# An attention and soft-MoE kernel: its decays computed in two halves at the opening, and its second layers taken in pairs of experts at the end

## The chip, the cores and the metric

The kernel runs on one core of a Trainium2 chip. The metric is the device time of one execution in microseconds (us), the median of three runs. Engines are called as the profile calls them: PE is TensorE's matmul and PEld its weight load, DVE is VectorE, ACT is ScalarE, POOL is GpSimd, and SP is SyncE, which issues every DMA of this kernel in one order.

## What is computed

The input is attention over 8 batches and 8 heads of 576 positions by 64, with a decay, and a soft mixture of 8 experts with 4 slots each on its output:

```python
log_f = np.log(np.clip(f, 0.0001, 1.0))
cum = np.cumsum(log_f, axis=-1)
scores = np.where(causal, -1e9, scale * q @ k.T + cum[:, :, :, None] - cum[:, :, None, :])
attn = softmax(scores) @ v                      # x: 4608 tokens x 512
logits = x @ phi                                # 4608 x 32 slots
slot_input = softmax_over_tokens(logits).T @ x  # 8 experts x 4 slots x 512
for e in range(8):
    slot_out[e] = np.maximum(slot_input[e] @ w1[e], 0.0) @ w2[e]
out = softmax_over_slots(logits) @ slot_out     # 4608 x 512, f32, 9.44 MB
```

## The kernel before

The order of work on each engine is the written order of the program; the framework adds the semaphores. All arithmetic is f32 or fp32r (f32 rounded for TensorE's fast path). Where more exactness is wanted, a number is used as a rounded part (hi) and the remaining part (lo).

**Opening (0 to about 26 us).** `f` (64 rows of 576) lands in `PTS`. DVE clips it (L548), ACT takes its logarithm (L549), DVE sums it along the row by a scan (L553), rounds the sums (L562) and takes the remaining part (L563, L564). ACT and DVE put sum rows into `WA[0]`, and fill rows into `YA[0]`. The keys and queries of pair 0 are in `RAW[0]`; `round_k` (L183) rounds a head's keys into `WA`, `round_q` (L188) its queries into `YA`, both on ACT. `dup_k` (L199) and `dup_q` (L203) are DMAs that copy these into `WB` and `YB`; `low_k` (L209) and `low_q` (L214) on POOL then write the remaining parts beside them. `s1` (L230) multiplies queries by keys for the row maxima, `tops` (L244, L246) takes the maxima on DVE, `s2` (L283, L284) makes the transposed scores with the maximum in them, `expo` (L290) their exponentials on ACT, `s3` (L315) the products with the values, `norm` (L330 to L335) the division. `warm` (L516) are matmuls on constants.

**Middle.** 32 pairs of heads run through a software pipeline of these steps; weights of the experts are loaded between them.

**End (from about 325 us).** `mlp1` and the first half of the second layers (`mlp2(e, 0)`, 16 matmuls each) run while weights still arrive. The output has two column halves of 256. For a half n, `gathered(n)` copies the sum of all experts out of PSUM, `slots(n)` adds up the four parts by a matmul with `srep`, and `halve(n)` makes the rounded and remaining part in `SO`. `blocks(n0, n1, half)` makes one or two blocks of 128 tokens by 256 columns, copies them out of PSUM on ACT and DVE in turn (L1071), and issues their DMA to the output (L1073), 256 KB for two blocks. There are 36 blocks in each half. Half 0's blocks are interleaved with the eight `mlp2(e, 1)`, which make half 1, and with the transposes of later batches' weights (`more`, L723). Of half 1, all blocks stand behind `halve(1)`.

Of the kernel before, what the change touches and what calls it, by code (L numbers as in the profile page):

```python
# [15 lines left out]
B, H, S, D = 8, 8, 576, 64  # L16
NE, SPE, DM, DF = 8, 4, 512, 1024
# [4 lines left out]
NBLK = 5  # L22
EPS = 1e-9

WARM = (11, 1)

CUM = ((64, 96), (64, 65), (64, 65))
TOP = (97, 66, 66)
# [41 lines left out]
SIDES = [[x for n in zip(units(h, 0, range(4)), units(h, 1, range(4))) for x in n] for h in range(2)]  # L70
LAST = [units(h, h, (4,)) for h in range(2)]
# [3 lines left out]
def attn_softmoe(ctx: ExitStack, tc: tile.TileContext, qk, v, f, phi, w1, w2, cst, out):  # L75
    nc = tc.nc
# [21 lines left out]
    YA, WA, YB, WB = {}, {}, {}, {}  # L98
# [204 lines left out]
    def blank(h):  # L303

        t = pv[h][:, 0:325].rearrange("p (t e) -> p t e", e=65)
        lanes = slice(64 * (1 - h), 64 * (1 - h) + 64)
        nc.vector.memset(t[lanes, 4, 0:64], 0.0)
        nc.vector.memset(t[lanes, 4, 64:65], 1.0)
        return t

    def s3(g, todo):
        for h, t, u, c in todo:
            r = queries(t, u)
            at = pt_col(c, 64 * r)
# [7 lines left out]
    def norm(i):  # L322
        if not head(i):
            return
        g, h = divmod(i, 2)
        b, p = divmod(g, NPAIR)
        x, o = xtile(b, p // 2), pvv[h]
        at = 128 * (p % 2) + 64 * h
        rl = small.tile([P, NBLK], F32, name=f"rl{i}", tag="rl")
        nc.vector.tensor_scalar_add(rl, o[:, :, 64], EPS)  # L330
        nc.vector.reciprocal(rl, rl)
        rl = rl.rearrange("p (t o) -> p t o", o=1)
        for ts in (slice(0, NBLK),) if i < NH - 1 else (slice(0, NBLK, 4), slice(1, 4)):
            to = x[:, ts, at : at + 64]
            nc.vector.tensor_tensor(to, o[:, ts, 0:64], rl[:, ts].broadcast_to(list(to.shape)), op=ALU.mult)  # L335
# [177 lines left out]
    def warm(n, a, w=192):  # L513

        for _ in range(n):
            nc.tensor.matmul(ring[0][:, 0:w], a[:, 0:128], a[:, 0:w], start=True, stop=True)  # L516
# [18 lines left out]
        nc.vector.memset(t[64:128, 448:512], 0.0)  # L535

    fill = V.rearrange("p a t c -> p (a t c)")[:, 0:1280].bitcast(F32R)
    nc.vector.memset(fill[0:1].bitcast(F32), -1.0)
    for h in range(2):
        nc.scalar.mul(fill[32:34, 640 * h : 640 * h + 640], fy[32:34], -8.0)  # L540
    warm(WARM[0], fy)
    nc.gpsimd.memset(WA[0][64:96].bitcast(F32), 0.0)
    nc.gpsimd.memset(YA[0][64:98].bitcast(F32), -8.0)
    nc.gpsimd.memset(WA[0][96:98].bitcast(F32), -1.0)
    nc.gpsimd.memset(YA[0][0:64, :, 0:64].bitcast(F32), 0.0)
    nc.gpsimd.memset(LG[:, 128:256], -1.0e30)
# [12 lines left out]
    dup_q(0, 0, 1)
    round_k(0, 1)  # L560

    nc.vector.tensor_copy(fp[lane, 0:S], fz)  # L562
    nc.vector.tensor_tensor(WA[0][96:97, 0:S], fz[0:1], fp[64:65, 0:S].bitcast(F32), op=ALU.subtract)  # L563
    nc.vector.tensor_tensor(fp[lane, S:], fz, fp[lane, 0:S].bitcast(F32), op=ALU.subtract)  # L564
    for m in (1, 2):
        nc.sync.dma_start(WA[m][66:67].bitcast(F32), fill[0:1, 0 : 2 * S].bitcast(F32))
        nc.sync.dma_start(YA[m][64:66].rearrange("c h s -> c (h s)").bitcast(F32), fill[32:34].bitcast(F32))
        if m == 1:
            dup_k(0, 1, 2)
            for c in range(2):  # L570
                nc.sync.dma_start(WA[1][64 + c : 65 + c].bitcast(F32), fp[65:98:32, S * c : S * c + S].bitcast(F32))
            nc.sync.dma_start(cumd.rearrange("b a c s -> (b a) (c s)"), fp[lane].bitcast(F32))
    for h in range(2):
        nc.scalar.copy(WA[0][64:65, S * h : S * h + S], fp[64 + 32 * h : 65 + 32 * h, 0:S])  # L574
    nc.scalar.copy(WA[0][96:97, S:], fp[96:97, S:])
    round_q(0, 1)
    dup_q(0, 1, 2)
    nc.scalar.activation(fin[:, 0:1], ones[:, 0:1], AF.Exp)
    for h in range(2):
        low_k(h)  # L580
        low_q(h)
    for m in (1, 2):
        nc.gpsimd.memset(YA[m][0:64, :, 0:64].bitcast(F32), 0.0)
    nc.gpsimd.memset(fin[0:1, 4:5], -1.0)
# [496 lines left out]
    mlp2(0, 1)
    slots(0)
    halve(0)
    mlp2(1, 1)
    more(5)
    ring += [po[0], bank[0]]
    runs = (((0, 2), (2, 4), (4, 6)), ((6, 8), (18, 20), (20, 22)), ((22, 24), (24, 26), (8, 9)), ((26, 27), (9, 11), (11, 13)), ((13, 15), (15, 17), (17, 18)), ((27, 29), (29, 31)), ((31, 33), (33, 35), (35, 36)))
    turns = ((5, 2), (2, 3), (3, 6), (6, 7), (7,), ())
    for e in range(2, NE):
        for n in runs[e - 2]:  # L1090
            blocks(*n, half[0])
        if e == 3:
            split(7, 0, 1)
        mlp2(e, 1)
        for n in turns[e - 2]:
            more(n)
    gathered(1)
    for n in runs[-1]:
        blocks(*n, half[0])
    slots(1)  # L1100
    halve(1)
# [45 lines left out]
```

## Time and profile before

| | |
|---|---|
| time, median of 3 runs | 384.83 us (384.54 to 384.94) |
| profiled execution, its own time | 384.53 us |
| its span, first to last instruction | 382.8 us |
| mean granted TensorE clock | 0.989 |
| busy: PE, DVE, ACT, POOL | 96%, 74%, 71%, 67% |
| instructions | 15236 |

The profiled execution lies 0.30 us below the median; 1.7 us of its time are outside the span. Busy shares are means over stages with different limits: in the middle PE is busy nearly always, and in the last eight fortieths of the span the DMA engines are.

### The profile page before, as it was taken

The numbers are of one execution on the slowest core, as the hardware profiler recorded it, in microseconds if no ns is written. First come the engines' busy times: TensorE is split into PE (matmuls) and PEld (weight loads), VectorE is DVE, ScalarE is ACT, GpSimd is POOL, SyncE is SP. The second block draws the span as 40 slices with busy tenths as digits, with TensorE's granted clock in tenths as the row PEclk, the third lists the DMA queues.
The fourth block names the chain that finished last, engine by engine and source line by source line (L and its number), as shares of the span: only waits on it lengthen the run. The fifth ranks groups of instructions, "written<-read, shape, count | busy, mean of one in ns | idle before, by whom it ended". The sixth has DMA issues, their size and how long they took to land.

```text
span 382.8 us, 15236 instructions
## 1 busy us (share of the span) xinstructions
PE 365.8 (96%) x5904; PEld 328.5 (86%) x5904; DVE 285.0 (74%) x1078; ACT 270.8 (71%) x656; POOL 257.0 (67%) x364
## 2 busy tenths in 40 slices
PE   7999999999999999999999999999999999999950
PEld 7899999999999999999999999999999986556650
DVE  7878887887888888888888888888888636442670
ACT  8969887878787878787878787878787653112450
POOL 4987887878797879787978797879787941010000
PEclk9999999999999999999999999999999999999995
DMA  6785878677768777778777777777777889999998
GB/s 209 202 200 158 240 231 272 197 221 214 236 188 242 206 233 210 219 205 235 214 218 215 224 212 221 216 220 217 218 217 210 264 290 395 411 406 374 313 330 293
DMA packets 37480, 93.72 MB, mean 245 GB/s; under 512 B 4458, under 2 KB 14368, under 8 KB 37408
## 3 DMA queue, kind: packets, MB, share of 16 engines
q1 hardware_dynamic: 37408, 92.75, 78.6%
q8 instruction: 46, 0.75, 0.8%
q14 instruction: 26, 0.21, 0.2%
HBM read 63.93 MB, written 9.73 MB: 192 GB/s over the span
## 4 chain that ended last, share of the span: by engine, by line
PE 91%; DVE 2%; ACT 1%; DMA 1%; issue 1%; POOL 0%; DVEq 0%; POOLq 0%; ACTq 0%
PE pv L315 25%; PE ring L283 15%; PE s L230 13%; PE ring L284 13%; PE pv L342 4%; PE lg L389 3%; PE pv L992 2%; PE ds L480 2%; PE ring L961 2%; PE pv L961 2%; PE ring L992 2%; PE ring L1070 1%; PE ring L480 1%; DMA PTS<-in_f 1%; PE more L1070 1%
## 5 line engine op out<-in xcount | busy, mean ns | idle before, releaser
L290 ACT ACTIVATE PTS<-ring 128x320 f32<-128x320 f32 (+2 forms) x256 | 119.4, 500 | 37.6 <-PE ring L284 29.9
L283 PE MATMUL ring<-YA,WA 67*128 67x320 f32 (+9 forms) x384 | 119.0, 324 | 0.0
L246 DVE CUSTOM_DVE_ANT_0 s<-s,mask 128x320 f32<-128x320 f32 (+3 forms) x256 | 109.5, 446 | 6.1 <-PE s L230 0.7
L284 PE MATMUL ring<-YB,WB 128*128 128x320 f32 (+4 forms) x384 | 110.5, 296 | 0.0
L315 PE MATMUL pv<-V,PTS 128*64 128x65 f32 x3200 | 101.9, 223 | 0.1
L315 PEld LDWEIGHTS pv<-V,PTS 128*64 128x64 f32 x3200 | 96.9, 138 | 3.0 <-issue 1.3
L230 PE MATMUL s<-WA,YA 66*128 66x288 f32 (+9 forms) x384 | 97.9, 311 | 1.0 <-ACT WA L574 0.6
L209 POOL TENSOR_TENSOR WB<-RAW,WB 64x576 fp32r<-64x576 f32 x64 | 90.7, 1417 | 10.3 <-DMA YA<-V 5.1
L214 POOL TENSOR_TENSOR YB<-RAW,YA 64x576 fp32r<-64x576 f32 x64 | 89.7, 1421 | 2.6
L283 PEld LDWEIGHTS ring<-YA,WA 67*128 67x128 f32 (+3 forms) x384 | 69.0, 181 | 5.4 <-issue 2.1
L284 PEld LDWEIGHTS ring<-YB,WB 128*128 128x128 f32 (+1 forms) x384 | 70.0, 182 | 0.0
L230 PEld LDWEIGHTS s<-WA,YA 66*128 66x128 f32 (+1 forms) x384 | 62.9, 190 | 6.5 <-ACT WA L574 0.8
L246 DVE DVE_READ_ACCUMULATOR2_ANT MT<- 128x1 fp32r x310 | 44.0, 142 | 0.0
L301 POOL TENSOR_SCALAR_AFFINE_SELECT PTS<-PTS 128x128 f32<-128x128 f32 (+1 forms) x128 | 31.3, 265 | 17.8 <-ACT PTS L290 14.7
L183 ACT CAST WA<-RAW 64x576 fp32r<-64x576 f32 x64 | 40.2, 669 | 3.7 <-DMA RAW<-in_qk 2.8
L298 POOL TENSOR_SCALAR_AFFINE_SELECT PTS<-PTS 128x384 f32<-128x384 f32 x64 | 33.3, 521 | 12.8 <-ACT PTS L290 7.4
L188 ACT CAST YA<-RAW 64x576 fp32r<-64x576 f32 x64 | 40.8, 669 | 0.4
L246 DVE CUSTOM_DVE_ANT_0 s<-s,mask,MT 128x288 f32<-128x288 f32 x62 | 32.6, 526 | 10.0 <-PE s L230 1.4
L342 PE MATMUL pv<-cs,X 128*128 128x128 f32 x155 | 36.5, 272 | 0.0
L335 DVE TENSOR_TENSOR X<-pv,rl 128x320 f32<-128x320 f32 (+1 forms) x65 | 31.5, 486 | 2.4 <-DMA YA<-mr 0.3
L330 DVE TENSOR_SCALAR rl<-pv 128x5 f32<-128x5 f32 x64 | 10.5, 164 | 26.4 <-PE pv L315 21.2
L244 DVE TENSOR_REDUCE MT<-s 128x1 fp32r<-128x288 f32 x62 | 28.0, 451 | 0.5
(257 smaller groups left out, 382.3 us busy)
## 6 DMA issues: line engine op xcount, KB each, us to landing
w<-in_w SPq DMA_DIRECT2D x45, 512.0 KB
RAW<-in_qk SPq DMA_DIRECT2D x31, 576.0 KB
V<-in_v SPq DMA_DIRECT2D x32, 325.0 KB
YB<-YA SPq DMA_DIRECT2D x30, 288.0 KB
WB<-WA SPq DMA_DIRECT2D x30, 288.0 KB
p<-in_w SPq DMA_DIRECT2D x6, 512.0 KB
out<-RAW SPq DMA_DIRECT2D x12, 256.0 KB
out<-p SPq DMA_DIRECT2D x10, 256.0 KB
```

The lines of the kernel that those rows point to most:

```text
L183: nc.scalar.copy(WA[g % 3][0:64, S * h : S * h + S], RAW[g % 3][64:128, h])
L188: nc.scalar.copy(YA[g % 3][0:64, h, 64:640], RAW[g % 3][0:64, h])
L209: nc.gpsimd.tensor_tensor(t[0:64], RAW[g % 3][64:128, h], t[64:128].bitcast(F32), op=ALU.subtract)
L214: nc.gpsimd.tensor_tensor(YB[g % 2][64:128, h], RAW[g % 3][0:64, h], YA[g % 3][0:64, h, 64:640].bitcast(F32), op=ALU.subtract)
L230: nc.tensor.matmul(t[:, o : o + w], ya[0:m, h, 128 * blk : 128 * blk + 128], wa[0:m, j0 : j0 + w], start=True, stop=True)
L246: nc.vector.tensor_tensor_reduce(out=t[:, o : o + w], in0=t[:, o : o + w], in1=mask[:, m0 : m0 + w], scale=1.0, scalar=top.bitcast(F32) if ...
L283: nc.tensor.matmul(o, wa[0:m, j0 : j0 + n], ya[0:m, h, 64 + i0 : 64 + i0 + w], start=True, stop=False)
L284: nc.tensor.matmul(o, wb[:, j0 : j0 + n], yb[:, h, i0 : i0 + w], start=False, stop=True)
L290: nc.scalar.activation(PT[i % 2][:, SEG_O[bank] : SEG_O[bank] + at], t[:, 0:at], AF.Exp, scale=0.125)
L298: nc.gpsimd.affine_select(d3, d3, pattern=[[0, 3], [1, 128]], compare_op=ALU.is_ge, fill=0.0, base=0, channel_multiplier=-1)
L315: nc.tensor.matmul(pvv[h][64 * u : 64 * u + 64, t, :], PT[h][:, at : at + 64], V[:, g % 2, c, 65 * h : 65 * h + 65], start=(c == 0), stop= ...
L342: nc.tensor.transpose(pm[:, 0:128], x[:, t, 128 * (p % 2) : 128 * (p % 2) + 128], ident)
```

## The change

Opening:
- The clip, the logarithm and the scan are done in two column halves of 288. The second scan starts from the last sum of the first. Two memsets of DVE stand ahead of the clip now.
- The fill rows of `YA[0]` are written by ACT rather than POOL, and the fill data for the other tiles are spread over 9 and 20 partitions.
- Nine warm matmuls stand at the start rather than 11.
- The load of the next pair's keys and queries (`load_qk(1)`, 576 KB) is issued behind the first `dup_k` and `dup_q` rather than ahead of them.
- The queries of head 1 are rounded on POOL, between `low_k(0)` and `low_q(0)`, rather than on ACT. ACT's copy of a sum row (L574 before, L566 now) stands ahead of `round_k(0, 1)`.
- `first(2, 2)` stands before the last part of head 0's `s2`; `norm(0)` stands behind `first(4, 3)`, and `s3` of head 1 is not split any more.

End:
- `gathered` makes a rounded part (ACT) and a remaining part (DVE) in two column halves of 128, and POOL copies `srep` beside them. `slots` is two fp32r matmuls (hi and lo) rather than one f32 matmul. `halve` does its two steps for each column half of 128.
- The second layers of half 1 run in pairs of experts, `runs` regroups the blocks in four groups, and `more` does four transposes groups at a time. `gathered(1)` stands right behind `mlp2(7, 1)`, ahead of the group of blocks from 27 on; `slots(1)` and `halve(1)` stand before the block pair (33, 35).

```diff
-    load_qk(1)
...
     for h in range(2):
-        nc.scalar.mul(fill[32:34, 640 * h : 640 * h + 640], fy[32:34], -8.0)
+        nc.scalar.mul(YA[0][64:98, h], fy[64:98], -8.0)
...
-    nc.gpsimd.memset(YA[0][64:98].bitcast(F32), -8.0)
...
-    nc.vector.tensor_scalar(fx, fx, 1e-4, 1.0, op0=ALU.max, op1=ALU.min)
-    nc.scalar.activation(fx, fx, AF.Ln)
...
-    nc.vector.tensor_tensor_scan(fz, fy[lane, 0:S], fx, 0.0, ALU.mult, ALU.add)
+    parts = slice(0, S // 2), slice(S // 2, S)
+    for n in parts:
+        nc.vector.tensor_scalar(fx[:, n], fx[:, n], 1e-4, 1.0, op0=ALU.max, op1=ALU.min)
+        nc.scalar.activation(fx[:, n], fx[:, n], AF.Ln)
+    for n, start in zip(parts, (0.0, fz[:, S // 2 - 1 : S // 2])):
+        nc.vector.tensor_tensor_scan(fz[:, n], fy[lane, n], fx[:, n], start, ALU.mult, ALU.add)
...
     dup_k(0, 0, 1)
     dup_q(0, 0, 1)
-    round_k(0, 1)
+    load_qk(1)
...
+    nc.scalar.copy(WA[0][64:65, 0:S], fp[64:65, 0:S])
+    round_k(0, 1)
...
-    round_q(0, 1)
+    low_k(0)
+    nc.gpsimd.tensor_copy(YA[0][0:64, 1, 64:640], RAW[0][0:64, 1])
     dup_q(0, 1, 2)
     nc.scalar.activation(fin[:, 0:1], ones[:, 0:1], AF.Exp)
-    for h in range(2):
-        low_k(h)
-        low_q(h)
+    low_q(0)
+    low_k(1)
+    low_q(1)
...
     s3(0, SIDES[0][20:] + LAST[0])
-    norm(0)
     first(4, 1)
-    s3(0, LAST[1] + SIDES[1][:8])
     first(4, 2)
     first(4, 3)
-    s3(0, SIDES[1][8:])
+    norm(0)
+    s3(0, LAST[1] + SIDES[1])
...
+    parts = [slice(128 * n, 128 * n + 128) for n in range(2)]
+    room = [last[0][:, 0:640], CW[0].rearrange("p t o r s -> p (t o r s)")]
+
     def gathered(n):
 
-        nc.vector.tensor_copy(so[:, half[n]], po[n][:, 0:256])
+        nc.gpsimd.tensor_copy(room[n][:, 512:640], srep)
+        for c in parts:
+            hi, lo = room[n][:, c], room[n][:, 256 + c.start : 256 + c.stop]
+            nc.scalar.copy(hi, po[n][:, c])
+            nc.vector.tensor_tensor(lo, po[n][:, c], hi.bitcast(F32), op=ALU.subtract)
 
     def slots(n):
-        nc.tensor.matmul(pr[n], srep, so[:, half[n]], start=True, stop=True)
+        for k in range(2):
+            nc.tensor.matmul(pr[n], room[n][:, 512:640], room[n][:, 256 * k : 256 * k + 256], start=(k == 0), stop=(k == 1))
 
     def halve(n):
-        nc.scalar.copy(SO[:, half[n]], pr[n])
-        nc.vector.tensor_tensor(SO[64:128, half[n]], pr[n][64:128], SO[64:128, half[n]].bitcast(F32), op=ALU.subtract)
+        for c in parts:
+            to = SO[:, 256 * n + c.start : 256 * n + c.stop]
+            nc.scalar.copy(to, pr[n][:, c])
+            nc.vector.tensor_tensor(to[64:128], pr[n][64:128, c], to[64:128].bitcast(F32), op=ALU.subtract)
...
-    runs = (((0, 2), (2, 4), (4, 6)), ((6, 8), (18, 20), (20, 22)), ((22, 24), (24, 26), (8, 9)), ((26, 27), (9, 11), (11, 13)), ((13, 15), (15, 17), (17, 18)), ((27, 29), (29, 31)), ((31, 33), (33, 35), (35, 36)))
...
+    runs = (
+        ((0, 2), (2, 4), (4, 6), (6, 8)),
+        ((18, 20), (20, 22), (22, 24), (24, 26), (8, 9), (26, 27)),
+        ((9, 11), (11, 13), (13, 15), (15, 17), (17, 18)),
+        ((27, 29), (29, 31), (31, 33), (33, 35), (35, 36)),
+    )
+    turns = ((5, 2), (3, 6), (7,), ())
...
+    for e in range(0, NE, 2):
+        mlp2(e, 1)
+        if e == 0:
+            slots(0)
+            halve(0)
+            ring += [po[0], bank[0]]
+        mlp2(e + 1, 1)
+        if e == NE - 2:
+            gathered(1)
+        for n in runs[e // 2]:
+            if n == (33, 35):
+                slots(1)
+                halve(1)
             blocks(*n, half[0])
-        if e == 3:
+        for n in turns[e // 2]:
+            more(n, 4)
+        if e == 0:
             split(7, 0, 1)
```

The first place is POOL's start of the opening's remaining parts, before and then after, with the semaphores that each row waits for (WB and YB take the remaining parts, RAW_95 is pair 0, DMAHW is a DMA's).

```order
L209 TENSOR_TENSOR WB_92<-RAW_95,WB_92 64x576 [waits DMAHW6_49,DMAHW1_49]
L214 TENSOR_TENSOR YB_91<-RAW_95,YA_89 64x576 [waits Activation_49,Pool_49]
L209 TENSOR_TENSOR WB_92<-RAW_95,WB_92 64x576 [waits DMAHW2_49]
L214 TENSOR_TENSOR YB_91<-RAW_95,YA_89 64x576 [waits Activation_49]
L583 MEMSET YA_85 64x2x64
```

```order
L209 TENSOR_TENSOR WB_92<-RAW_95,WB_92 64x576 [waits DMAHW5_49,DMAHW1_49]
L580 CAST YA_89<-RAW_95 64x576 [waits DMAHW2_49]
L214 TENSOR_TENSOR YB_91<-RAW_95,YA_89 64x576 [waits Activation_49,Pool_49]
L209 TENSOR_TENSOR WB_92<-RAW_95,WB_92 64x576 [waits DMAHW2_49]
L214 TENSOR_TENSOR YB_91<-RAW_95,YA_89 64x576 [waits Pool_49]
```

The rounding of head 1's queries (L580) now stands behind POOL's first instruction, which waits for the DMA of `dup_k`.

The second place is ACT at the first fold of the end, before and then after (ring and more are PSUM banks, SO takes the folded slots, RAW_95 an output block).

```order
L1055 CAST SO<-ring_151 128x256 [waits PE_49]
L733 CAST cT<-more_5701 128x256 [waits PE_49]
L1071 COPY RAW_95<-more_5702 128x512 [waits DMAHW3_49,DVE_49,PE_49]
L1071 COPY RAW_96<-ring_150 128x512 [waits DMAHW2_49,DVE_49,PE_49]
L733 CAST cT_6032<-ring_152 128x256 [waits DVE_49,PE_49]
```

```order
L1057 CAST cT_6033<-ring_152 128x128 [waits PE_49]
L1057 CAST cT_6033<-ring_152 128x128 [waits DVE_49]
L1067 CAST SO<-ring_151 128x128 [waits PE_49]
L1067 CAST SO<-ring_151 128x128 [waits DVE_49]
L1083 COPY RAW_95<-more_5702 128x512 [waits DMAHW3_49,PE_49]
```

The second column half's rounding on ACT now waits for DVE, at `gathered` (L1057) and again at `halve` (L1067).

The third place is DVE at the second fold, before and then after (w and p are output blocks).

```order
L1049 COPY ctok<-pv_148 128x256 [waits PE_49]
L1071 COPY w_131<-ring_150 128x512 [waits PE_49,Activation_49]
L1071 COPY w_138<-ring_152 128x256 [waits PE_49]
L1056 TENSOR_TENSOR SO<-pv_149,SO 64x256 [waits Activation_49]
L1071 COPY RAW_95<-more_5702 128x512 [waits DMAHW7_49,PE_49]
```

```order
L1058 TENSOR_TENSOR cw_5634<-pv_148,cw_5634 128x128 [waits Activation_49] x2
L1083 COPY w_130<-more_5703 128x512 [waits PE_49]
L1083 COPY w_131<-ring_150 128x512 [waits PE_49]
L1068 TENSOR_TENSOR SO<-pv_149,SO 64x128 [waits Activation_49] x2
L1083 COPY w_138<-ring_151 128x256 [waits PE_49]
L1083 COPY RAW_95<-more_5703 128x512 [waits DMAHW7_49,PE_49]
```

Behind `gathered(1)` now stand four and a half output pieces of half 0, where one and a half stood before; the first of them is copied by DVE behind the two subtractions.

## Rows read from the trace of the kernel before

**Rows 1.** The page: granted clock by fortieths of the span, and the chain's shares.

```profile
PEclk9999999999999999999999999999999999999995
...
PE 91%; DVE 2%; ACT 1%; DMA 1%; issue 1%; POOL 0%; DVEq 0%; POOLq 0%; ACTq 0%
```

**Rows 2.** The chain at the opening: start us, us, what.

```profile
0.81 2.64 DMA PTS<-in_f
...
3.47 0.92 DVE PTS L548
...
4.42 0.69 ACT PTS L549
...
5.13 1.36 DVE PTS L553
...
6.52 0.47 DVE PTS L562
...
10.68 0.54 PE s L230 x3
```

**Rows 3.** The timeline of the opening: start us, us, engine line op, [idle before <-releaser].

```profile
5.81 0.52 SPq L199 DMA_DIRECT2D WB<-WA  x1
...
7.20 1.36 ACT L574 CAST WA<-PTS 1x576 fp32r<-1x576 f32 x2
...
9.85 1.41 POOL L209 TENSOR_TENSOR WB<-RAW,WB 64x576 fp32r<-64x576 f32 x1 [5.09 <-DMA YA<-V]
```

**Rows 4.** Groups by line and form: busy us, mean ns of one.

```profile
L1071 DVE COPY p<-ring 128x512 f32<-128x512 f32 x4 | 2.7, 684 | 0.1
...
L1071 DVE COPY w<-ring 128x256 f32<-128x256 f32 x2 | 0.8, 416 | 0.0
...
L335 DVE TENSOR_TENSOR X<-pv,rl 128x128 f32<-128x128 f32 x1 | 0.3, 292 | 0.0
...
L730 ACT CAST cT<-more 128x128 fp32r<-128x128 f32 x2 | 0.4, 269 | 0.4 <-PE more L721 0.4
...
L298 POOL TENSOR_SCALAR_AFFINE_SELECT PTS<-PTS 128x384 f32<-128x384 f32 x64 | 33.3, 521 | 12.8 <-ACT PTS L290 7.4 <-ACT XTS L375 1.2 <-POOL WB L209 0.3
...
L432 POOL COPY LDT<-LDT 32x64 f32<-32x64 f32 x7 | 1.6, 226 | 0.4
```

**Rows 5.** The chain around the first products with the values.

```profile
23.07 1.19 PE pv L315 x26
...
24.82 0.85 PE pv L315 x24
```

**Rows 6.** The timeline of the end: start us, us, engine line op.

```profile
347.89 0.42 DVE L1049 COPY ctok<-ring 128x256 f32<-128x256 f32 x1 [3.83 <-PE ring L992]
...
348.61 0.70 PE L1052 MATMUL ring<-ctok,cs 128*128 128x256 f32 x2
...
349.35 0.37 ACT L1055 CAST SO<-ring 128x256 fp32r<-128x256 f32 x1 [5.89 <-PE ring L1052]
349.75 0.43 DVE L1056 TENSOR_TENSOR SO<-ring,SO 64x256 fp32r<-64x256 f32 x1 [1.44 <-ACT SO L1055]
...
363.38 0.43 DVE L1049 COPY ctok<-pv 128x256 f32<-128x256 f32 x1 [0.35 <-PE pv L992]
...
366.03 0.59 ACT L1071 COPY w<-ring 128x512 f32<-128x512 f32 x1 [1.06 <-PE ring L1070]
```

**Rows 7.** The chain at the end: second layers without and with a switch, and blocks.

```profile
340.41 0.86 PE ring L992 x16
...
362.32 1.00 PE pv L992 x16
...
366.00 0.24 PE more L1070 x2
```

**Rows 8.** Windows of the end: us, busy time of each engine, granted clock, DMA share, GB/s.

```profile
378.00:381.00 3.00, 0.00 (x0) 0.00 (x0) 0.00 (x0) 0.00 (x0) 0.00 (x0) 0.50 1.02 343
381.00:382.80 1.80, 0.00 (x0) 0.00 (x0) 0.00 (x0) 0.00 (x0) 0.00 (x0) 0.50 0.23 77
```

More of the change, by code (lines that the diff above doesn't have):

```diff
@@ L23 @@
 EPS = 1e-9
-WARM = (11, 1)
+WARM = (9, 1)
 CUM = ((64, 96), (64, 65), (64, 65))
@@ L537, in attn_softmoe @@
     fill = V.rearrange("p a t c -> p (a t c)")[:, 0:1280].bitcast(F32R)
-    nc.vector.memset(fill[0:1].bitcast(F32), -1.0)
+    nc.vector.memset(fill[0:9, 0:128].bitcast(F32), -1.0)
     for h in range(2):
-        nc.scalar.mul(fill[32:34, 640 * h : 640 * h + 640], fy[32:34], -8.0)
+        nc.scalar.mul(YA[0][64:98, h], fy[64:98], -8.0)
+    for h in range(2):
+        nc.vector.memset(m2[h], -8.0)
+    pvv = [blank(h) for h in range(2)]
     warm(WARM[0], fy)
+    nc.gpsimd.memset(fill[32:52, 0:128].bitcast(F32), -8.0)
     nc.gpsimd.memset(WA[0][64:96].bitcast(F32), 0.0)
-    nc.gpsimd.memset(YA[0][64:98].bitcast(F32), -8.0)
     nc.gpsimd.memset(WA[0][96:98].bitcast(F32), -1.0)
@@ L547, in attn_softmoe @@
     nc.gpsimd.memset(EX[:, 192:256], 0.0)
-    nc.vector.tensor_scalar(fx, fx, 1e-4, 1.0, op0=ALU.max, op1=ALU.min)
-    nc.scalar.activation(fx, fx, AF.Ln)
-    for h in range(2):
-        nc.vector.memset(m2[h], -8.0)
-    pvv = [blank(h) for h in range(2)]
-    nc.vector.tensor_tensor_scan(fz, fy[lane, 0:S], fx, 0.0, ALU.mult, ALU.add)
+    parts = slice(0, S // 2), slice(S // 2, S)
[4 more added lines that the diff above has]
+        nc.vector.tensor_tensor_scan(fz[:, n], fy[lane, n], fx[:, n], start, ALU.mult, ALU.add)
     round_k(0, 0)
@@ L559, in attn_softmoe @@
     dup_q(0, 0, 1)
-    round_k(0, 1)
+    load_qk(1)
     nc.vector.tensor_copy(fp[lane, 0:S], fz)
     nc.vector.tensor_tensor(WA[0][96:97, 0:S], fz[0:1], fp[64:65, 0:S].bitcast(F32), op=ALU.subtract)
+    nc.scalar.copy(WA[0][64:65, 0:S], fp[64:65, 0:S])
+    round_k(0, 1)
     nc.vector.tensor_tensor(fp[lane, S:], fz, fp[lane, 0:S].bitcast(F32), op=ALU.subtract)
     for m in (1, 2):
-        nc.sync.dma_start(WA[m][66:67].bitcast(F32), fill[0:1, 0 : 2 * S].bitcast(F32))
-        nc.sync.dma_start(YA[m][64:66].rearrange("c h s -> c (h s)").bitcast(F32), fill[32:34].bitcast(F32))
+        nc.sync.dma_start(WA[m][66:67].bitcast(F32), fill[0:9, 0:128].bitcast(F32))
+        nc.sync.dma_start(YA[m][64:66].rearrange("c h s -> c (h s)").bitcast(F32), fill[32:52, 0:128].bitcast(F32))
         if m == 1:
@@ L572, in attn_softmoe @@
             nc.sync.dma_start(cumd.rearrange("b a c s -> (b a) (c s)"), fp[lane].bitcast(F32))
-    for h in range(2):
-        nc.scalar.copy(WA[0][64:65, S * h : S * h + S], fp[64 + 32 * h : 65 + 32 * h, 0:S])
+    nc.scalar.copy(WA[0][64:65, S:], fp[96:97, 0:S])
     nc.scalar.copy(WA[0][96:97, S:], fp[96:97, S:])
-    round_q(0, 1)
+    low_k(0)
+    nc.gpsimd.tensor_copy(YA[0][0:64, 1, 64:640], RAW[0][0:64, 1])
     dup_q(0, 1, 2)
     nc.scalar.activation(fin[:, 0:1], ones[:, 0:1], AF.Exp)
-    for h in range(2):
-        low_k(h)
-        low_q(h)
+    low_q(0)
+    low_k(1)
+    low_q(1)
     for m in (1, 2):
@@ L632, in attn_softmoe @@
     next(r1)
+    first(2, 2)
     s2(0, 3, 4, 5)
@@ L639, in attn_softmoe @@
     load_cum(2)
-    first(2, 2)
     first(2, 3)
@@ L1002, in attn_softmoe @@
     half = [slice(256 * n, 256 * n + 256) for n in range(2)]
-    so = ctok.rearrange("p b t s -> p (b t s)")[:, 0:DM]
     used = 0
@@ L1078, in more @@
             next(c[b])
-    gathered(0)
[L1081 to L1086, printed above, removed]
-    runs = (((0, 2), (2, 4), (4, 6)), ((6, 8), (18, 20), (20, 22)), ((22, 24), (24, 26), (8, 9)), ((26, 27), (9, 11), (11, 13)), ((13, 15), (15, 17), (17, 18)), ((27, 29), (29, 31)), ((31, 33), (33, 35), (35, 36)))
-    turns = ((5, 2), (2, 3), (3, 6), (6, 7), (7,), ())
-    for e in range(2, NE):
-        for n in runs[e - 2]:
+    runs = (
[4 rows of a table added]
+    )
+    turns = ((5, 2), (3, 6), (7,), ())
+    gathered(0)
+    for e in range(0, NE, 2):
[11 more added lines that the diff above has]
+                halve(1)
             blocks(*n, half[0])
-        if e == 3:
+        for n in turns[e // 2]:
+            more(n, 4)
+        if e == 0:
             split(7, 0, 1)
[L1094 to L1101, printed above, removed]
     ring += [po[1], bank[1]]
```

## The prediction

> **What bounds the kernel now.** I read the page first, then the chain of waits, then the timelines of the two stretches that the change touches, then windows of the end. Nine tenths of the chain that ended last are PE's [rows 1]: from the first scores to the last second layer, time that PE loses or wins goes to the end, whatever the other engines do. Two stretches differ. Before 10.7 us the chain has no PE: the load of f, the clip, the logarithm, the scan and the rounding follow each other on DVE and ACT with hardly a gap [rows 2], and nothing can start earlier than these end. At the end the output's DMA decides: in its last microseconds no engine works, and the DMA engines write 343 GB/s at a full share [rows 8]. A piece of two blocks is 256 KB (262,144 bytes), so 0.764 us. Data end at 381.00 + 77 x 1.80 / 343 = 381.40 us. Half 1's first piece is out of PSUM at 366.03 + 0.59 = 366.62 [rows 6]; its 18 pieces take 13.75 us, so 1.03 us pass from ready to first byte: 366.62 + 1.03 + 13.75 = 381.40. The reader should see that the end is set by when the last long unbroken train of pieces starts, and by how many pieces are in it.
>
> **Opening: the decays in halves.** A DVE copy of 512 columns takes 0.684 and one of 256 columns 0.416 us [rows 4], so about 0.15 us of an instruction don't shrink; the same follows for ACT from 0.59 and 0.37 [rows 6]. Halves are then 0.53 for the clip, 0.42 for the logarithm, 0.75 for the scan. With f landed at 3.45 [rows 2]: clips 3.47 to 4.00 and to 4.53, logarithms 4.03 to 4.45 and 4.56 to 4.98, scans 4.56 to 5.31 and to 6.06. Before, the scan ended at 6.49: 0.4 us won for the rounding, for ACT's row copy (before held to 7.20 behind a rounding that is now behind it [rows 3]) and for head 0's first scores.
>
> **Opening: what this runs into.** Head 1's scores (10.68 [rows 2]) need its rounded queries. These are now made by POOL behind its first `low_k`, which waits for `dup_k`: issued at 5.81, it let POOL start only at 9.85, after 5.09 us idle [rows 3]. Now ACT's rounding ends earlier and no 576 KB load is queued ahead, so issue at 5.70. Landing is bounded by f's 2.64 us from issue to use (8.35) and by the 4.04 us of before (9.75); I take the middle, 8.9, since the two loads of pair 0 and the constants are still ahead. `low_k` takes 1.41 [rows 3]. POOL's rounding of 64x576 isn't in the trace: below stands a 32x64 copy (0.23), above the two-input 64x576 (1.41); a line through 0.23 for 64 columns and 0.52 for 384 [rows 4] gives 0.70 for 576, which I take as nearest. Head 1 then starts at 8.9 + 1.41 + 0.70 + 0.04 = 11.05, 0.4 us later than before. With the ends of both bounds it is 10.4 to 12.6, so -0.3 to +1.9. Behind the waiting `low_k` on POOL stand `low_q(0)` (end 8.9 + 1.41 + 0.70 + 1.41 = 12.4; before 9.85 + 2 x 1.41 = 12.7), then head 1's parts. So the 0.4 us of the halves are not spent where they arise: head 0 is early, head 1 late, and PE takes them in order.
>
> **Opening: the rest.** Moving `norm(0)` and joining `s3` of head 1: 26 products took 1.19 and 24 took 0.85 on the chain [rows 5], 46 and 35 ns each; at the lower rate 0.3 are saved. `first(4, 3)` now has a bank of tops ahead of it, so I take -0.2 (0 to -0.5). Nothing for the smaller memsets, the fill rows on ACT (it waits for DVE there anyway), fewer warm matmuls (PE's clock was granted at nine tenths or more in every fortieth but the last [rows 1]), and the fill DMAs. The moved load adds one issue of about 0.5 us on SP ahead of the fills and the second `dup_k`; their readers stand behind three POOL instructions. If its 576 KB are late for the next pair's rounding, ACT waits, inside the upper bound. Opening: +0.4 - 0.2 = **+0.2 us** (-0.8 to +1.9).
>
> **End: the folds.** Before, `gathered` is one DVE copy of 0.42, hidden beside a second layer, and `halve` 0.37 on ACT, then 0.43 on DVE [rows 6]. Now each is ACT, DVE, ACT, DVE, because ACT's second part waits for DVE's first (the order shows the wait): 0.27 + 0.29 + 0.27 + 0.29 [rows 4], with four hand-overs of 0.03 to 0.04 (349.35 + 0.37 to 349.75 [rows 6]) **1.26 us**. If instead ACT's second part followed its first at once, the fold would be 0.27 + 0.27 + 0.29 and two hand-overs, 0.9 us. In the trace, DVE never starts on a bank before ACT is done with it (349.72, 349.75 [rows 6]), so it shows no overlap within one bank.
> The Trainium skill's page PSUM — Partial Sum Buffer, section "PSUM bank collisions raise a hardware error", says that two engines may not touch one bank in the same 32 partitions at once, reads and different columns included, and that the chip does not hold one back, so that a dependency is added. By it a fold is the 1.26 us; without it, 0.9. No run so far shows a collision.
>
> **End: PE up to the last second layer.** Before: 347.85 to 363.32 [rows 6, 7], 15.47 us. Now: idle before `slots`, 347.85 + 1.26 = 349.11 instead of 348.58, +0.53; `slots` as two matmuls at block rate (0.24 for two [rows 7]) instead of about 0.65, -0.4; `mlp2(1, 1)` runs to 350.4 and `halve` to 349.4 + 1.26 = 350.7, +0.3 (before, transposes filled this); 27 blocks rather than 31 ahead of `mlp2(7, 1)`, -4 x 0.12 = -0.5; second layers in pairs save a switch (1.00 against 0.86 [rows 7]) three times, -0.4. Sum -0.5: `mlp2(7, 1)` ends at **362.9**.
>
> **End: the train of pieces.** `gathered(1)` holds DVE and ACT to 362.9 + 1.26 = 364.1, and the copy of blocks 27 and 28 stands behind it on DVE: ready at 364.85. By then the queue has run dry: the first 13.5 pieces take 10.3 us from about 352.6, to 362.9. All that is left is 4.5 pieces of half 0 and 18 of half 1, 22.5 x 0.764 = 17.2 us, in one train: 364.85 + 1.03 + 17.2 = 383.1, against 381.40, **+1.7 us**. Half 1 can't be late: `halve(1)` ends near 365.7, and the 4.5 pieces last to 369.3. So the hold that stood before half 1 moves to 4.5 pieces earlier and lasts longer. Bounds: with no saving from pairs +2.1, with folds of 0.9 us +0.7, with folds that cost no more than before (no idle, 0.43) 0.
>
> **Sum.** 384.53 + 0.2 + 1.7 = **386.4 us** for the profiled execution, whose time is 0.30 below the median of 384.83; I give it unmoved. Against the median it is 1.6 us or 0.4% more. About 0.2% (0.77 us) is what a measurement of this kernel can tell from no change.
>
> **Rivals.**
> First, *the folds overlap*: ACT's second part does not wait in practice because DVE is already done. For it: DVE's part is as short as ACT's. Against it: DVE can only begin when ACT's first part ends. Then +0.7 and 384.53 + 0.2 + 0.7 = 385.4, no change by the bound above.
> Second, on the other side, *the folds are free and the opening wins*: for it speak the 0.4 us of the halves and the 0.5 us fewer of PE before the last second layer. With folds as cheap as before, `mlp2(7, 1)` ends at 362.0, the first piece is ready at 363.2, and 363.2 + 1.03 + 17.2 = 381.4: end +0. With `dup_k` landed by 8.4 and the saving at `s3`, the opening gives -0.7: 383.8, faster. It decides from a first piece at 363.2 or earlier.
> Third, *the gate on POOL*: `dup_k` lands as late as before and the rounding costs as much as the two-input form: opening +1.7, 384.53 + 1.7 + 1.7 = 387.9. For it: the 5.09 us that POOL idled. Against it: the load ahead of `dup_k` is gone.
> That the change doesn't do what it says (halves that PE's queue swallows, so that neither end moves) gives 384.5.
>
> **How the numbers follow.** Forecast 0.53 (own range 385.6 to 387.4), folds that overlap 0.14, free folds with a winning opening 0.13, the POOL gate 0.13, neither end moves 0.07. Slower than 385.6: the forecast and the gate, 0.66; within 0.2%: overlap and no move, less a little, 0.20; faster: 0.14. The range leaves out the free folds and the worst of the gate: 384.3 to 387.8.
>
> **What would show it.** Right: the scan's second half ends near 6.1; POOL's first `low_k` starts between 8.4 and 9.7, and PE's first scores of head 1 begin right behind its rounding; four steps of 0.27 to 0.30 at each fold, ACT's second waiting for DVE; PE idle ahead of `slots`; a DMA share well below 1 between 363 and 366, then 17.2 us without a gap. Wrong: ACT's two parts back to back; a share of 1 through 363 to 366, which would mean that pieces queue up behind the DMA and the late train costs nothing; or first exponentials more than 0.5 us earlier than before.

## The result and the profile after

The changed kernel takes 386.70 us (median of 13, 386.12 to 390.66) against 384.69 for the kernel before (13 runs beside it): a ratio of 1.0064, 95% interval 1.0046 to 1.0083. It is slower by about 2 us. The profiled execution took 387.12 us, with a span of 385.4 against 382.8.

The page of the changed kernel, granted clock by fortieths, and the shares of the chain [rows 1]:

```profile
PEclk9999999999999999999999999999999999999985
...
PE 89%; DVE 2%; ACT 2%; DMA 2%; POOL 1%; issue 1%; DVEq 0%; SPq 0%; ACTq 0%; POOLq 0%
PE pv L315 25%; PE ring L283 14%; PE s L230 13%; PE ring L284 13%; PE pv L342 4%; PE lg L389 3%; PE ds L480 2%; PE ring L964 2%; PE pv L964 2%; PE ring L995 2%; PE pv L995 2%; DMA WA<-cumd 1%; ACT PTS L290 1%; PE more L1082 1%; PE ring L1082 1%
```

New in the chain is a DMA, the load of the decay sums (`WA<-cumd`, 1%). PE's share fell from 91% to 89%; DMA, ACT and POOL gained 1% each.

Its timeline of the opening answers to [rows 2, 3] (start us, us, engine line op, [idle before <-releaser]):

```profile
4.38 1.69 DVE L555 TENSOR_TENSOR_SCAN PTS<-WB,PTS 64x288 f32<-64x288 f32 x2 [0.29 <-ACT PTS L553]
...
5.58 0.53 SPq L199 DMA_DIRECT2D WB<-WA  x1
...
6.79 0.60 SPq L174 DMA_DIRECT2D RAW<-in_qk  x1
7.51 0.90 SPq L570 DMA_DIRECT2D WA<-V  x1
...
8.05 1.41 POOL L209 TENSOR_TENSOR WB<-RAW,WB 64x576 fp32r<-64x576 f32 x1 [4.34 <-DMA WB<-WA]
...
9.52 0.66 POOL L580 CAST YA<-RAW 64x576 fp32r<-64x576 f32 x1
...
10.23 0.45 PEld L230 LDWEIGHTS s<-WA,YA 97*128 97x128 f32 x3 [0.28 <-POOL YA L580]
...
11.70 0.80 SPq L570 DMA_DIRECT2D WA<-V  x1
...
13.65 1.30 ACT L290 ACTIVATE PTS<-ring 128x448 f32<-128x448 f32 x3
...
15.25 0.37 SPq L178 DMA_DIRECT2D V<-in_v  x1
...
18.27 0.45 SPq L194 DMA_DIRECT2D WA<-cumd  x1
...
20.80 1.39 PE L315 MATMUL pv<-V,PTS 128*64 128x65 f32 x40 [0.93 <-POOL YB L214]
...
22.48 0.47 PE L230 MATMUL s<-WA,YA 66*128 66x320 f32 x2 [0.29 <-DMA WA<-cumd]
...
26.39 0.47 PE L283 MATMUL ring<-YA,WA 67*128 67x448 f32 x1
```

The same view of the kernel before:

```profile
3.49 0.43 SPq L174 DMA_DIRECT2D RAW<-in_qk  x1
...
7.09 0.59 SPq L566 DMA_DIRECT2D WA<-V  x1
...
10.38 0.83 PE L230 MATMUL s<-WA,YA 97*128 97x320 f32 x3
...
10.91 0.58 SPq L566 DMA_DIRECT2D WA<-V  x1
...
13.99 1.30 ACT L290 ACTIVATE PTS<-ring 128x448 f32<-128x448 f32 x3 [0.21 <-PE ring L284]
...
14.23 0.39 SPq L178 DMA_DIRECT2D V<-in_v  x1
...
20.13 1.39 PE L315 MATMUL pv<-V,PTS 128*64 128x65 f32 x40
...
21.45 0.50 PE L230 MATMUL s<-WA,YA 66*128 66x320 f32 x2
...
25.60 0.47 PE L283 MATMUL ring<-YA,WA 67*128 67x448 f32 x1
```

The scan ends at 6.07 rather than 6.49. POOL's `low_k` starts 2.5 us after the issue of `dup_k`, and head 1's scores start right behind POOL's rounding, at 10.23 against 10.38 before. The first exponentials start at 13.65; before it was 13.99. Then PE waits twice where it did not wait before, 0.93 us ahead of the first products with the values and 0.29 for the decay sums.

The row names POOL's L214 for the first wait, but the semaphores in the trace name the load of the values (L178): its last part lands at 20.67, and PE is let go at 20.70. Before, these were 19.47 and 19.50. In run 2 below, where the row names ACT, they are 20.64 and 20.67.

So PE, 0.34 us ahead at 13.65, is 0.67 behind at the first products, and 0.79 behind the products of pair 0 (26.39 against 25.60). When the end begins, its sum of half 0 is ready 1.14 us later (349.03 below against 347.89 [rows 6]). That last part comes in the middle, most of it in one step near 43 us that no wait in the rows explains.

The timeline of the end answers to [rows 6]:

```profile
349.03 0.27 ACT L1057 CAST cT<-ring 128x128 fp32r<-128x128 f32 x1 [4.43 <-PE ring L995]
349.33 0.29 DVE L1058 TENSOR_TENSOR cT<-ring,cT 128x128 fp32r<-128x128 f32 x1 [4.12 <-ACT cT L1057]
349.65 0.27 ACT L1057 CAST cT<-ring 128x128 fp32r<-128x128 f32 x1 [0.35 <-DVE cT L1058]
349.95 0.29 DVE L1058 TENSOR_TENSOR cT<-ring,cT 128x128 fp32r<-128x128 f32 x1 [0.33 <-ACT cT L1057]
...
350.02 0.66 PE L1062 MATMUL ring<-cT 128*128 128x256 f32 x2 [0.19 <-issue]
...
363.84 0.27 ACT L1057 CAST cw<-pv 128x128 fp32r<-128x128 f32 x1 [1.48 <-PE pv L995]
...
364.76 0.29 DVE L1058 TENSOR_TENSOR cw<-pv,cw 128x128 fp32r<-128x128 f32 x1 [0.33 <-ACT cw L1057]
...
364.97 0.68 DVE L1083 COPY w<-more 128x512 f32<-128x512 f32 x1
```

ACT, DVE, ACT, DVE: each waits for the other, and a fold takes 1.21 us. The first piece of the last group is copied behind it, ready at 365.65.

Windows of the end answer to [rows 8] (granted clock, DMA share and GB/s are the last three):

```profile
365.50:366.00 0.50, 0.35 (x3) 0.14 (x2) 0.50 (x2) 0.27 (x1) 0.00 (x0) 1.00 0.65 225
366.00:366.50 0.50, 0.00 (x0) 0.00 (x0) 0.47 (x2) 0.00 (x0) 0.00 (x0) 1.00 0.06 20
366.50:367.00 0.50, 0.00 (x0) 0.00 (x0) 0.17 (x2) 0.39 (x2) 0.00 (x0) 1.00 0.83 264
...
367.50:368.00 0.50, 0.50 (x4) 0.50 (x4) 0.15 (x1) 0.00 (x1) 0.00 (x0) 0.50 1.02 352
...
383.50:384.00 0.50, 0.00 (x0) 0.00 (x0) 0.00 (x0) 0.00 (x0) 0.00 (x0) 0.50 0.77 266
```

The queue is nearly dry from 365.7 to 366.6. Then the train runs without a gap to 383.5 + 266 x 0.5 / 343 = 383.89. That is 2.49 us later than before: 1.14 from the middle and 1.35 from the end itself.

### The profile page after: what moved, and what is told of

Read it like the earlier page. It is cut to its first block, busy times and chain, and to the rows that moved or that the text cites. A ratio compares the mean times of both kernels' runs of the same rounds, so it can differ in the third digit from the quotient of the medians.

```text
span 385.4 us, 15243 instructions
## 1 busy us (share of the span) xinstructions
PE 366.3 (95%) x5900; PEld 329.9 (86%) x5900; DVE 284.1 (74%) x1084; ACT 271.7 (70%) x662; POOL 256.9 (67%) x367
## 4 chain that ended last, share of the span: by engine, by line
PE 89%; DVE 2%; ACT 2%; DMA 2%; POOL 1%; issue 1%; DVEq 0%; SPq 0%; ACTq 0%; POOLq 0%
PE pv L315 25%; PE ring L283 14%; PE s L230 13%; PE ring L284 13%; PE pv L342 4%; PE lg L389 3%; PE ds L480 2%; PE ring L964 2%; PE pv L964 2%; PE ring L995 2%; PE pv L995 2%; DMA WA<-cumd 1%; ACT PTS L290 1%; PE more L1082 1%; PE ring L1082 1%
## 5 line engine op out<-in xcount | busy, mean ns | idle before, releaser
L214 POOL TENSOR_TENSOR YB<-RAW,YA 64x576 fp32r<-64x576 f32 x64 | 89.8, 1421 | 2.6
L188 ACT CAST YA<-RAW 64x576 fp32r<-64x576 f32 x63 | 40.1, 669 | 0.4
L330 DVE TENSOR_SCALAR rl<-pv 128x5 f32<-128x5 f32 x64 | 10.5, 163 | 26.9 <-PE pv L315 21.9
```

## The experiments

All were timed in five rounds beside the kernel before. "Cost" is the difference of the medians; the 95% interval is that of the ratio. The sum column says how much later than before (347.89 [rows 6]) half 0's sum was ready in the profiled execution: what the opening and the middle lost.

| run | cost, us | ratio, 95% interval | sum of half 0, us |
|---|---|---|---|
| 1, end alone | +1.30 | 1.0022 to 1.0048 | +0.05 |
| 2, opening alone | +1.05 | 1.0011 to 1.0037 | +1.45 |
| 3, opening, early load | +2.75 | 1.0047 to 1.0082 | +3.17 |
| 4, late load alone | +0.73 | 1.0013 to 1.0033 | +0.81 |
| 5, halves only | +0.06 | 0.9996 to 1.0014 | +0.18 |
| 6, end, folds whole | +0.30 | 1.0000 to 1.0018 | +0.15 |
| 7, end, old folds in pairs | +0.16 | 0.9995 to 1.0013 | +0.67 |
| 8, old end, new folds | +1.51 | 1.0030 to 1.0055 | +0.29 |
| 9, opening, rounding first | +1.21 | 1.0024 to 1.0048 | +1.06 |
| 10, the same, early load | +0.44 | 1.0000 to 1.0017 | +1.51 |
| 11, whole, both mends | +0.47 | 1.0000 to 1.0017 | +0.48 |
| 12, as 9, pair 2 earlier | +0.89 | 1.0014 to 1.0045 | +1.68 |

Openings alone and mended ones differ from execution to execution: run 2 ranged from 384.83 to 387.33, run 10 from 384.40 to 386.07, whose profiled execution was the slowest. Their sums of half 0 are therefore those of one execution, and the medians count.

**Runs 1 and 2: the parts alone.** All hunks of the diff up to `s3` of pair 0 are the opening, the rest is the end.

> The opening of before with the new end. If the two parts add up, the end alone costs what its own stretch shows: the last matmul of half 0's sum to the end of the output data took 383.9 - 349.83 = 34.05 us against 381.4 - 348.68 = 32.7, so +1.3 to +1.4 us, 386.0 to 386.1. If the late end came instead from PE arriving 1.1 us later (the out queue then being the same), the end alone gives +0 to +0.4, at most 385.1.

> The new opening with the end of before. If PE's delay of 1.13 us at the last pair is passed on whole, +1.1 us, 385.8. If the end's out queue hides part of it, or the delay is one that only some executions have, +0.3 to +0.6.

Both parts cost, +1.30 and +1.05 us; together 2.35, and the whole change 2.01. The end is as its own stretch showed. The opening's delay is passed on whole: 1.45 us at the sum of half 0 and 1.43 us in the profiled time (385.96 against 384.53).

**Runs 3 and 4: the load of pair 1.** Run 3 is run 2 with the load back in its old place; run 4 is the kernel before with only this move:

```diff
     nc.sync.dma_start(cs, cst[:, 0:258])
-    load_qk(1)
...
     dup_q(0, 0, 1)
+    load_qk(1)
     round_k(0, 1)
```

> The new opening with the 576 KB load of pair 1 issued in its old place, ahead of the first copies; end of before. Theory that the late load leaves the DMA queues idle at 5.5 to 7 us and piles up the loads at 15 to 24 us: the waits for V and for the sum rows near 20 and 22 us go, and the opening is -0.3 to 0 us, 384.4 to 384.7. Rival, that POOL's rounding of head 1 and the order of the products with the values cost the time: it stays at +0.8 to +1.1, since neither is touched, or grows if the copy of head 0's keys is late again behind the load.

> The kernel before with only this change: the 576 KB load of pair 1 is issued behind the first two copies rather than ahead of them. Theory of the late load: +0.8 to +1.2 us, 385.5 to 385.9. Rival (other parts of the opening cost it): within 0.3 us of before, or faster, since head 0's copy of keys lands earlier.

Run 4 costs 0.73 us, a little under what the late-load theory gave. But run 3 is the slowest of all: the early load is worse, not better. Its waits of PE (us in total, times, longest), and POOL's first row:

```profile
PE s L230 <- POOL YA L580: 1.9, 1, 1.9
```

```profile
10.02 1.40 POOL L209 TENSOR_TENSOR WB<-RAW,WB 64x576 fp32r<-64x576 f32 x1 [6.31 <-DMA WB<-WA]
```

With 576 KB ahead of it, `dup_k` lands at 10.0 rather than 8.05, POOL's rounding of head 1 stands behind it, and PE waits 1.9 us. The theory of the late load was wrong for this run, and the rival's last clause came true: the copy of head 0's keys is late behind the early load. The late load costs, and it is the price for POOL's rounding standing where it does.

**Run 5: halves only.** The kernel before with the clip, logarithm and scan in halves, ACT's row copy ahead of `round_k(0, 1)`, and DVE's long memset moved to POOL.

```diff
-    nc.vector.tensor_scalar(fx, fx, 1e-4, 1.0, op0=ALU.max, op1=ALU.min)
-    nc.scalar.activation(fx, fx, AF.Ln)
...
-    nc.vector.tensor_tensor_scan(fz, fy[lane, 0:S], fx, 0.0, ALU.mult, ALU.add)
+    for n in parts:
+        nc.vector.tensor_scalar(fx[:, n], fx[:, n], 1e-4, 1.0, op0=ALU.max, op1=ALU.min)
+        nc.scalar.activation(fx[:, n], fx[:, n], AF.Ln)
+    for n, start in zip(parts, (0.0, fz[:, S // 2 - 1 : S // 2])):
+        nc.vector.tensor_tensor_scan(fz[:, n], fy[lane, n], fx[:, n], start, ALU.mult, ALU.add)
...
-    round_k(0, 1)
...
+    nc.scalar.copy(WA[0][64:65, 0:S], fp[64:65, 0:S])
+    round_k(0, 1)
```

> The kernel before with the decays in two halves and ACT's row copy ahead of its rounding, and nothing else: the load of pair 1 in its old place, head 1's queries rounded on ACT, the old end. Theory that the opening lost by the late load and by POOL's rounding, not by the halves: first exponentials 0.35 us earlier and, since PE is the chain from there on, -0.3 us, 384.4 to 384.6. Rival, that whatever is won before 14 us is lost again to the loads between 15 and 25 us (they don't come earlier): within 0.15 us of before.

The rival held: 0.06 us, no change. The timeline shows why before 14 us: ACT's rows.

```profile
7.01 0.67 ACT L566 CAST WA<-PTS 1x576 fp32r<-1x576 f32 x1 [0.58 <-DVE PTS L564]
7.70 0.67 ACT L183 CAST WA<-RAW 64x576 fp32r<-64x576 f32 x1
...
9.78 0.67 ACT L188 CAST YA<-RAW 64x576 fp32r<-64x576 f32 x1
...
14.18 0.54 ACT L290 ACTIVATE PTS<-ring 128x448 f32<-128x448 f32 x1
```

ACT now idles 0.58 us for the scan and does its rounding afterwards, so head 1's queries (L188) are rounded at 9.78, against 9.41 before; ACT is full from 7 to 10.5 us. Before, ACT rounded head 1's keys at 6.51, while DVE was still at the sums, and had no such gap. So the moved row copy takes back what the earlier scan gives, and run 5 does not show what the halves are worth without that move.

**Runs 6, 7 and 8: folds or regrouping.** Run 6 is the new end with each fold in one piece (the diff against the new end; `halve` likewise). Run 7 takes the new `runs`, `turns` and loop and keeps `gathered`, `slots` and `halve` of before; run 8 takes these three functions of the change and keeps the old loop.

```diff
     def gathered(n):
         nc.gpsimd.tensor_copy(room[n][:, 512:640], srep)
-        for c in parts:
-            hi, lo = room[n][:, c], room[n][:, 256 + c.start : 256 + c.stop]
-            nc.scalar.copy(hi, po[n][:, c])
-            nc.vector.tensor_tensor(lo, po[n][:, c], hi.bitcast(F32), op=ALU.subtract)
+        hi, lo = room[n][:, 0:256], room[n][:, 256:512]
+        nc.scalar.copy(hi, po[n][:, 0:256])
+        nc.vector.tensor_tensor(lo, po[n][:, 0:256], hi.bitcast(F32), op=ALU.subtract)
```

> The new end on the old opening, with each fold in one piece: ACT 256 columns, then DVE 256 columns, for both the gathering and the halving; slots still as two fp32r matmuls, second layers in pairs. Theory of ACT and DVE alternating on one bank: a fold is 0.37 + 0.43 + two hand-overs = 0.87 us instead of 1.21, so the last train starts 0.34 us earlier, and PE's idle time ahead of the first folds shrinks by as much: end at +0.6 to +0.9, 385.5 to 385.8. Rival, that the regrouping in pairs costs the time: as the end alone, 386.1 to 386.2.

> The new end's regrouping in pairs of experts on the old opening, with the old folds (gathering by one DVE copy, one f32 matmul, halving in one piece). Theory of the folds: the gathering takes 0.43 again, nothing idles ahead of slots, the last train starts where it did for 18 pieces but with 4.5 more in it, so end at 0 to +0.3, 384.8 to 385.2. Rival of the regrouping: the queue runs dry in front of run 4 whatever the folds cost, +0.9 to +1.3, 385.8 to 386.2.

> The old end's order (experts one by one, old runs) with the new folds in halves. Theory of the folds: PE idles 0.5 us ahead of the first slots and half 1's fold takes two times 1.21 instead of 0.43 and 0.87, so half 1's train of 18 pieces starts 1.0 to 1.4 us later less 0.3 for the faster slots: +0.9 to +1.3, 385.8 to 386.2. Rival of the regrouping: without pairs the folds are hidden beside the blocks, 0 to +0.4.

The folds are the cause: +1.51 us with them in the old order, +0.16 without them in the new one. Run 1 against run 6 prices the column halves alone, 1.00 of the 1.30 us. That is more than I expected, since three folds, not two, stand ahead of the last train (`gathered(0)`, `halve(0)`, `gathered(1)`): from the start of the first to the first piece of the last group it is 16.62 us in the changed kernel (349.03 to 365.65) and 15.46 in run 6 (348.04 to 363.50). Run 6's `gathered(1)`, DVE's rows:

```profile
362.48 0.42 DVE L1054 TENSOR_TENSOR cw<-pv,cw 128x256 fp32r<-128x256 f32 x1 [1.45 <-ACT cw L1053]
362.82 0.68 DVE L1077 COPY w<-more 128x512 f32<-128x512 f32 x1
```

It starts with ACT at 362.07 and is done at 362.90, so 0.83 us instead of 1.21. Run 7's `gathered(1)` is one copy again, and the first piece follows at once:

```profile
362.76 0.42 DVE L1049 COPY ctok<-pv 128x256 f32<-128x256 f32 x1 [1.05 <-PE pv L992]
363.17 0.69 DVE L1071 COPY w<-more 128x512 f32<-128x512 f32 x1
```

In run 8 half 1's first blocks wait for the second of two alternating folds:

```profile
364.11 0.27 ACT L1055 CAST cw<-pv 128x128 fp32r<-128x128 f32 x1 [0.45 <-PE pv L992]
...
366.90 0.29 DVE L1066 TENSOR_TENSOR SO<-pv,SO 64x128 fp32r<-64x128 f32 x1 [0.33 <-ACT SO L1065]
367.25 0.51 PE L1080 MATMUL ring<-SO,cT 128*128 128x256 f32 x2 [1.50 <-DVE SO L1066]
```

From the sum (364.11) to the blocks (367.25) it takes 3.1 us; before it took 2.1, from 363.38 [rows 6] to this row:

```profile
365.49 0.51 PE L1070 MATMUL ring<-SO,cT 128*128 128x256 f32 x2 [0.92 <-DVE SO L1056]
```

**Runs 9 to 12: mends.** Run 9 is run 2 with POOL's rounding ahead of `low_k(0)`, run 10 also has the load early, run 11 is the whole change with the mends of runs 6 and 10. Run 12 is run 9 with `load_qk(2)` issued behind the copy of the decay sums.

```diff
     dup_q(0, 0, 1)
+    nc.gpsimd.tensor_copy(YA[0][0:64, 1, 64:640], RAW[0][0:64, 1])
...
     low_k(0)
-    nc.gpsimd.tensor_copy(YA[0][0:64, 1, 64:640], RAW[0][0:64, 1])
```

```diff
             nc.sync.dma_start(cumd.rearrange("b a c s -> (b a) (c s)"), fp[lane].bitcast(F32))
+            load_qk(2)
```

> The new opening, old end, with POOL's rounding of head 1's queries ahead of its first remaining part (it then waits for no copy of head 0's keys); the load of pair 1 stays late. Theory that the late load is what costs the new opening 1.05 us as long as it stays behind the copies: +0.7 to +1.1, 385.4 to 385.8. Rival, that POOL's place costs it: 384.6 to 384.9.

> As the run before, and the load of pair 1 in its old, early place; old end. Theory that the two parts of the opening bite each other (the early load delays the copy for which POOL's rounding waits, the late load delays all later loads): with the rounding ahead of the wait, the early load costs nothing, first exponentials near 13.65 against 13.99, -0.2 to -0.35 us, 384.35 to 384.55. Rival, that the loads between 15 and 25 us bound PE whatever comes before: within 0.15 us of before.

> The whole changed kernel with both mends: POOL's rounding first and the load early, and the folds in one piece each. If opening and end add up: the mended opening (-0.3) and the end with whole folds (+0.3), 384.6 to 384.9. If the opening's gain doesn't reach the end: 385.0 to 385.2.

> The new opening with POOL's rounding first, load of pair 1 late, old end, and one move more: the load of pair 2 (576 KB) is issued right behind the copy of the decay sums, near 11 us rather than 14.4, where the DMA share is 0.08 to 0.7. Theory that the late load costs by piling up pair 2's keys, the values and the sum rows at 15 to 22 us: PE no longer waits 1.1 us for the values, and the time falls from 385.9 to 384.4 to 384.9. Rival, that the pile is not what PE waits for (the order of issue on SP, or head 1's second copy, now behind this load): no better than 385.5.

In run 9 the rounding waits for no copy, and the opening still costs 1.21 us; PE's second longest wait is now for the values:

```profile
PE pv L315 <- DMA V<-in_v: 1.1, 1, 1.1
```

With the load early (run 10) most of this goes, 1.21 to 0.44, but nothing is won: the two theories for run 10 gave -0.3 and 0, and it came out above both. Its profiled execution shows `dup_k` landing late again, and now POOL's remaining parts hold the first exponentials:

```profile
10.96 1.41 POOL L209 TENSOR_TENSOR WB<-RAW,WB 64x576 fp32r<-64x576 f32 x1 [4.44 <-DMA WB<-WA]
12.44 1.41 POOL L214 TENSOR_TENSOR YB<-RAW,YA 64x576 fp32r<-64x576 f32 x1
```

They end at 13.85, and the first exponentials start at 14.42. Runs 2, 3, 9 and 10 are the four ways of two choices. With the load late, POOL's place makes little difference (+1.05 and +1.21); with the load early it decides (+2.75 and +0.44). Runs 9 and 10 differ in the load alone, and by 0.77 us, as run 4 does from before by 0.73. Run 11, both mends, is 1.5 us faster than the change and at 1.0000 to 1.0017 no better than before. No version here beats the kernel before.

Run 12 did not empty the pile. The values' buffer also holds the fill rows, whose DMAs stood behind the moved load, so the values were issued at 17.35 rather than 15.06, and PE waited for a copy of queries and for the values:

```profile
17.51 0.47 PE L284 MATMUL ring<-YB,WB 128*128 128x448 f32 x1 [0.79 <-DMA YB<-YA]
21.43 1.39 PE L315 MATMUL pv<-V,PTS 128*64 128x65 f32 x40 [1.00 <-DMA V<-in_v]
```

So it tells nothing about what an earlier second load is worth by itself.

## Why the prediction was right, and where it was not

**The time and its sign** were right: 386.4 forecast, 386.70 measured. The two terms were less so: +0.2 for the opening (measured +1.05 alone) and +1.7 for the end (+1.30 alone). Their errors, 0.85 too little and 0.4 too much, partly cancel, so that 386.4 came so close is in part luck.

**The folds** were right in mechanism and nearly in size: four steps of 0.27 to 0.29, 1.21 us where I had 1.26, and with the folds taken out the end is back at +0.16. The rule of the Trainium skill's page PSUM — Partial Sum Buffer, section "PSUM bank collisions raise a hardware error", that two engines' accesses to one bank are kept apart by a dependency even at different columns, agrees with the timeline: DVE's first part ends at 349.62 and ACT's second starts at 349.65, and so at each of the four folds. No run shows what would happen without the dependency.

**The end's sum** was oversized by 0.35 us at two places. `mlp2(7, 1)` ended at 363.82, which without the 1.14 us from the opening and the middle is 362.68, not 362.9; and from there to the first piece it took 1.83 us rather than 1.95. In front of `slots` two errors cancel. PE idled 0.19 us rather than 0.53, because the first of the two matmuls needs only ACT's parts and starts (350.02) before DVE is done (350.24). The second waits for DVE, so that `slots` took 0.59 us (350.02 to 350.61) and not 0.24. The train itself, 365.65 + 1.03 + 17.2 = 383.88, ended at 383.89. The dry queue ahead of it lasted 0.9 us and not 3, since the pieces before it left gaps near 357 and 361 us; that moves nothing, as the train starts with its first piece. And behind `gathered(1)` two and a half pieces stood before: one and a half are DVE's, and ACT copied one more.

**The step that failed** is in the opening's rest: "The moved load adds one issue of about 0.5 us on SP ahead of the fills and the second `dup_k`; their readers stand behind three POOL instructions", priced at nothing. I followed the first reader of each transfer, but not the transfers that queue behind. From the first `dup_k` to the load of the values SP issues with hardly a pause: 8.42 us before (5.81 to 14.23), 9.67 now (5.58 to 15.25). The moved load takes 0.72 of the difference (6.79 to 7.51); before, it was issued at 3.49, and SP paused behind it until 5.81. The two fill DMAs L570, now over nine partitions, take another 0.53 (0.90 + 0.80 against 0.59 + 0.58), and I had put them at nothing too. So the values are issued 1.02 us later, land 1.20 later, and PE waits 0.93.

The load alone, moved, costs 0.73 us (run 4): the sum rows are issued at 18.6 as before, but PE waits 0.4 us for them. In run 9, where POOL's rounding waits for no copy, the late load and the rest of the opening cost 1.21. No run moves the fill DMAs alone.

**Head 1** I had wrong in sign, and I misread its start before: 10.68 [rows 2] is a later step of the chain, and the timeline has head 1's first scores at 10.38. POOL started 2.5 us after the issue of `dup_k`, at 8.05, below the bound of 2.64 that I took from f's load and below the 8.4 to 9.7 that I named as a sign. Head 1 started 0.15 us early rather than 0.4 late. The gate on POOL that I kept as a rival is real, but with the early load (run 3: 1.9 us of waiting), not with the late one.

**The joined products** gave the 0.2 us that I took: PE's delay falls from 1.01 (22.95 against 21.94, in front of them) to 0.79 behind them.

**The halves** do what they say (scan 0.42 us earlier; 0.34 of it is left at the first exponentials), and none of it reaches the end: in run 5 ACT is the bound behind them, in run 10 POOL's remaining parts, in run 9 the load of the values.

**Open**: how the opening's cost divides. That the late load costs is shown (run 4, and run 9 against 10), and so is what PE waits for behind it: the values (0.93 to 1.1 us) and the sum rows (0.29 to 0.8). Why the sum rows, issued earlier than before (18.27 against 18.61), take 4.1 us to land rather than 2.7 is not shown; run 12 could not take the pile of loads away. Nor is the 0.44 us that run 10 still costs; the longer issue of the fill DMAs could be part of it, which no run tests.

## What to carry to other kernels

Splitting work between two engines by columns won nothing here, where both read the same PSUM bank, and cost 1 us: look in the instruction order whether the second part of the first engine waits for the second engine, and count the steps in a row. At an end that is one train of output DMAs, count what is left to write from the last time that the queue runs dry; whatever holds the first piece of that train is the end. A load moved behind small copies in one issue order is paid for by what is issued later: add up the issue times, and follow the queue past the first reader.

## What was not expected of the hardware

- The same middle does not take the same time in every execution. In run 7, whose opening and middle are those of the kernel before, the first exponentials started at the same 13.98, but half 0's sum was ready 0.67 us later in the profiled execution. Nearly all of it comes in one step, between 53 and 61 us; why isn't known.
- In the changed kernel PE idles from 365.9 to 367.25, and the granted clock is at 0.50 (1.2 GHz) from 367.5 to 370.5, while half 1's blocks are made; then it is 1.00 again. No cost shows here: the DMA share stays near 1 through these microseconds, so the blocks are made as fast as they are written.
- Two executions of the changed kernel took 389.93 and 390.66 us at a mean clock of 0.977, against 0.985 to 0.989 in the others. No trace of them was taken, so where they lost 3 us isn't known.
